# One 128-partition load of the Toeplitz operand in place of two 64-partition loads

## The chip, the cores and the metric

The kernel runs on one core of a Trainium2 chip. The metric is the device time of one execution in microseconds (us). A profile of one execution was taken by the hardware profiler; "the span" is the time from its first to its last instruction. Engines: PE is TensorE, DVE is VectorE, ACT is ScalarE, POOL is GpSimd, SP is SyncE, whose queue issues every transfer of this kernel. Sixteen DMA engines move the data.

## The reference

Two branches read the same x (2048 positions, 448 channels, bfloat16) and are mixed by a gate per position:

```python
g = _sigmoid((x * gate_w).sum(-1, keepdims=True))
a = _A_ref(x, A_wq, A_wk, A_wv, A_wo)      # attention, 16 heads of 28, one shared key and value head
b = _B_ref(x, B_A_re, ..., B_Dskip)        # per channel d: y = causal convolution of x[:, d] with K[d, :], plus x * Dskip
return g * a + (1 - g) * b

# in _B_ref: the convolution's kernel K, 448 channels x 2048 lags, and the convolution itself by FFT
P = jnp.exp(logdA[:, :, None] * l[None, None, :])
K = jnp.einsum("dn,dnl,dn->dl", Cc, P, dB).real
y = irfft2(rfft2(x padded) * rfft2(K padded))[..., :L]
```

## The kernel before, in words

**The scheduler.** All work is given to `Prog` as operations with an engine, an estimated duration, what they read and write, and a priority. `Prog.schedule` simulates the engines with these estimates and writes down a fixed order for each engine; `Prog.emit` adds semaphore waits. At run time every engine works through its own list strictly in order, SP's list of transfers too. In the simulation a transfer takes 60 ns of SP for each of its parts, and then a time that follows from the pair `(rows, bytes per row)`; for a load of T that pair is (128, 8192) before and after the change.

**Attention.** `main` runs over 4 x 4 x 16 x 4 tiles (query chunk, group, key tile, head in the group) in 410 groups of three or two tiles. For each group PE computes scores (L905), ACT takes the exponential (L915) and PE multiplies with the values (L929). After 64 tiles `norm` divides by the sum of the exponentials, which goes through three small transfers (denT, R_scratch, rdenB) on SP's queue and three DVE operations (L874, L879, L883).

**The convolution.** It is done without an FFT, in 28 chunks of 16 channels, spread evenly over the attention's groups by `chunk_step`:

- `tables` (DVE) and `kgen` (PE, L764) compute the chunk's K for all lags; DVE copies it to `kstg` (L774), and four transfers write it to `KP_scratch` in DRAM, one row of 2112 elements for each channel; four channels are interleaved element by element, so that neighbouring lags of one channel are 4 elements apart.
- `tload(gi)` loads for four channels the operand T, a Toeplitz matrix laid out by overlapping reads: partition r of a half holds 4096 elements (8192 bytes) that begin r positions (of 4 elements) later than those of partition 0. There are three buffers for T (`NTR = 3`), and 112 loads in all, 4 per chunk. A load waits for the chunk's transfers to `KP_scratch` and until the buffer's last matmuls are done. It is two transfers of 64 partitions: partitions 64 to 127 begin 4096 elements, or 1024 lags, after partitions 0 to 63.
- `conv(c)` runs two chunks behind `tables(c)`. For each load it issues 64 small matmuls (L820) in 8 operations, of low priority, so that they stand between the attention's matmuls. Their other operand is U, x in blocks of 64 positions; the sum runs over the 128 partitions of U and T. DVE then takes the result out of PSUM (L828), and `ytr` (L797, L804) transposes it and adds it to the output O.

**U** is loaded once (`uload`, 48 transfers of 64 partitions): partitions 0 to 63 hold blocks in one order, partitions 64 to 127 hold the blocks 16 further on, since the second half of T lies 1024 lags away. Where partitions 0 to 63 have no block, U must be zero; a memset in `consts` (L394) sees to that.

**In time.** The first 84 us prepare x, the parameters and the first attention groups. Loads of T run from 84.5 us to 745 us. What remains is attention, the output projection and the stores of O.

Of the kernel before, what the change touches and what calls it, by code (L numbers as in the profile page):

```python
# [11 lines left out]
P = 128  # L12

S = 2048
D = 448
# [8 lines left out]
KPW = 2112  # L24
# [20 lines left out]
def dram(t, off, dims):  # L45
    return bass.AP(tensor=t.tensor, offset=t.offset + off, ap=[list(d) for d in dims])
# [240 lines left out]
class Kernel:  # L287
# [79 lines left out]
    def consts(self):  # L367
        pg = self.pg
        V = lambda b, off, n: b.v(0, P, off, [[1, n]])
        pg.op("pool", lambda e: e.memset(V(self.ident, 0, P), 1.0), 200, wr=["id"])  # L370
        pg.op("pool", lambda e: e.affine_select(
            out=V(self.ident, 0, P), in_=V(self.ident, 0, P), compare_op=ALU.is_equal, fill=0.0,
            base=0, pattern=[[-1, P]], channel_multiplier=1), 300, rd=["id"], wr=["id"])
        sm = self.small
        pg.op("dve", lambda e: e.tensor_reduce(V(sm, 0, 1), self.ident.v(0, P, 28, [[32, 4]]), AX.X, ALU.max),
              100, rd=["id"], wr=["s0"])
        pg.op("dve", lambda e: e.tensor_scalar(V(sm, 1, 1), V(sm, 0, 1), -0.5, 0.5, ALU.mult, ALU.add),
              100, rd=["s0"], wr=["s1"])
        pg.op("dve", lambda e: e.tensor_scalar(V(sm, 2, 1), V(sm, 0, 1), 0.5, 0.5, ALU.mult, ALU.add),
              100, rd=["s0"], wr=["s2"])  # L380
        pg.op("dve", lambda e: e.memset(V(sm, 3, 1), 0.5 * math.pi), 60, wr=["hpi"])
        for c, val in enumerate([-1.0, 1.0, 1.0, -1.0]):
            pg.op("pool", lambda e, c=c, val=val: e.memset(V(self.sgn, c, 1), val), 60, wr=["sgn"])
        ms = lambda buf, n, val, key: pg.op("dve", lambda e: e.memset(V(buf, 0, n), val), 60 + n / 3.8, wr=[key])
        ms(self.Wq, NT * 512, 0.0, "Wq")
        ms(self.Wk, NT * P, 0.0, "Wk")
        pg.op("dve", lambda e: e.memset(self.Wk.v(96, 32, 3 * P + 28, [[32, 4]]), 1.0), 60, wr=["Wk"])
        pg.op("dve", lambda e: e.memset(self.Wk.v(96, 16, 3 * P + 28, [[32, 4]]), 0.0), 60, wr=["Wk"])
        pg.op("dve", lambda e: e.memset(self.xT.v(96, 32, 3 * S, [[1, S]]), 1.0), 600, wr=["xT3a", "xT3b"])
        ms(self.Wo, NT * D, 0.0, "Wo")  # L390
        ms(self.Wb, P, 0.0, "Wb")
        pg.op("dve", lambda e: e.memset(self.vaug.v(0, P, 28, [[32, 16]]), 1.0), 80, wr=["va"])
        pg.op("dve", lambda e: e.memset(self.vaug.v(0, P, 29, [[32, 16], [1, 3]]), 0.0), 80, wr=["va"])
        pg.op("dve", lambda e: e.memset(self.U.v(0, 64, 16 * D, [[1, 16 * D]]), 0.0), 2000, wr=["Uz"])  # L394
        an = self.anti.v(0, 32, 0, [[32, 4], [1, 32]])
        pg.op("pool", lambda e: e.memset(an, 1.0), 100, wr=["anti"], pr=4)
        pg.op("pool", lambda e: e.affine_select(out=an, in_=an, compare_op=ALU.is_equal, fill=0.0, base=-31,
                                                pattern=[[0, 4], [1, 32]], channel_multiplier=1), 300,
              rd=["anti"], wr=["anti"], pr=4)
        pg.op("dve", lambda e: e.memset(V(self.kstg, 0, 256), 0.0), 100, wr=[("kst", 0)])  # L400
# [40 lines left out]
    def uload(self):  # L441
        pg, x = self.pg, self.ins["A_x"]
        for k in range(3):
            lst = []
            for p in range(16):
                if k == 0:
                    hb, pos, blk = 0, p, 15 - p
                else:
                    hb, pos, blk = 1, p + 16 * (k - 1), 31 - p - 16 * (k - 1)
                lst.append((self.U.v(64 * hb, 64, pos * D, [[1, D]]), dram(x, 64 * blk * D, [[D, 64], [1, D]])))  # L450
            pg.dma(lst, (1024, 896), f"u{k}", rd=["sw", "Uz"], wr=["U"], pr=2)

    def bank(self, b, bf=False):
# [327 lines left out]
    def tload(self, gi):  # L781
        pg = self.pg
        s = gi % self.NTR
        c = gi // 4
        pg.dma([(self.T.v(64 * h, 64, s * 4096, [[1, 4096]]),
                 dram(self.KP, 4 * gi * KPW + 4096 * h, [[4, 64], [1, 4096]])) for h in range(2)],
               (128, 8192), f"T{s}", rd=[("KP", c), "pad"], wr=[("T", s)], pr=1)

    def ytr(self, c):
# [246 lines left out]
```

## Time and profile before

| | |
|---|---|
| median of 3 runs | 817.01 us (816.29 to 826.21) |
| the profiled execution's own time | 816.14 us |
| its span | 814.4 us |
| mean granted clock of TensorE | 0.747 |
| busy: PE / DVE / ACT | 636.6 / 530.4 / 506.6 us |
| DMA queue of SP (q1) | 132.60 MB, 72.5% of 16 engines |
| issues of T | 224 of 512 KB |

How to read the lines that follow. "L820" is line 820 of the kernel. A wait is written `engine line <- releaser: us in total, times, longest us`. In the groups, `out<-in` names the buffers, then the shapes, the count, and busy time with the mean of one. PEclk is the clock that TensorE was granted, as a share of full speed. The DMA share is the mean busy share of the 16 DMA engines and can go a little over 1 where packets overlap. A releaser called "issue" means that the engine waited for nothing that the profile shows. Durations come from the one profiled execution.

### The profile page before, as it was taken

The page shows a single profiled execution, that of the slowest core. Times are in us where ns is not written, and L with a number is a line of the kernel's source. Part 1 is how long each engine was busy: PE and PEld are TensorE (multiplying, and loading weights), DVE is VectorE, ACT ScalarE, POOL GpSimd, SP SyncE. Part 2 cuts the span into 40 slices and gives each one's busy share as a digit, 9 for nine tenths or more (in the row PEclk, how much of TensorE's full clock was granted, in tenths as well). Part 3 has the DMA queues.
Part 4 walks back from the last instruction along what each step waited for, and adds up shares of the span by engine and source line. Part 5 has one row for each costly group of instructions (what it writes and reads, how often), then busy time and mean ns, then how long its engine had stood idle before and what let it go on. Part 6 is the DMA issues. An engine that isn't in the chain of part 4 may idle for free.

```text
span 814.4 us, 25556 instructions
## 1 busy us (share of the span) xinstructions
PE 636.6 (78%) x11649; PEld 307.7 (38%) x11649; DVE 530.4 (65%) x1156; ACT 506.6 (62%) x430; POOL 1.6 (0%) x12
## 2 busy tenths in 40 slices
PE   6378888797889878878789978778878988866852
PEld 4212243344334443444443543343433544433211
DVE  7999677956678684956769786755759867300101
ACT  3368667675665755756577856555658766654850
POOL 0000000000000000000000000000000000000000
PEclk9655668687677976868887967775868987876656
DMA  8032883899947899599948799796983799999003
GB/s 209 1 78 59 179 189 85 191 203 209 224 97 165 190 221 225 126 222 210 225 110 201 166 218 221 165 215 136 228 195 95 159 205 214 209 210 214 20 2 103
DMA packets 46036, 134.23 MB, mean 165 GB/s; under 512 B 14968, under 2 KB 29544, under 8 KB 31592
## 3 DMA queue, kind: packets, MB, share of 16 engines
q1 hardware_dynamic: 45928, 132.60, 72.5%
q8 instruction: 91, 1.49, 0.9%
q14 instruction: 17, 0.14, 0.1%
HBM read 128.57 MB, written 3.86 MB: 163 GB/s over the span
## 4 chain that ended last, share of the span: by engine, by line
DMA 38%; PE 38%; DVE 9%; SPq 6%; ACT 5%; issue 4%
DMA T<-KP_scratch 30%; PE psS L820 10%; PE psS L905 9%; PE psB L929 9%; SPq L102 6%; PE psX L764 5%; ACT expT L915 5%; DMA denT<-acc 4%; PE psX L640 2%; DMA rdenB<-R_scratch 2%; DMA R_scratch<-denT 1%; DMA KP_scratch<-kstg 1%; PE psX L851 1%; DVE tab L725 1%; DVE acc L874 1%
## 5 line engine op out<-in xcount | busy, mean ns | idle before, releaser
L915 ACT ACTIVATE expT<-psS 128x1536 bf16<-128x1536 f32 (+1 forms) x410 | 490.7, 1237 | 254.2 <-PE psS L905 247.9
L820 PE MATMUL psS<-T,U 128*32 128x64 bf16 (+15 forms) x7168 | 191.1, 257 | 95.3 <-DMA T<-KP_scratch 70.5
L929 PE MATMUL psB<-expT,vaug 128*32 128x512 bf16 x1024 | 207.4, 494 | 23.4 <-ACT expT L915 18.5
L820 PEld LDWEIGHTS psS<-T,U 128*32 128x32 bf16 (+15 forms) x7168 | 155.5, 182 | 174.3 <-issue 76.6
L905 PE MATMUL psS<-qT,kT 29*128 29x512 bf16 x1024 | 198.1, 484 | 4.2 <-issue 3.8
L905 PEld LDWEIGHTS psS<-qT,kT 29*128 29x128 bf16 x1024 | 39.8, 94 | 147.4 <-issue 146.6
L929 PEld LDWEIGHTS psB<-expT,vaug 128*32 128x32 bf16 x1024 | 53.0, 116 | 71.3 <-ACT expT L915 53.9
L725 DVE TENSOR_TENSOR tab<-tab,mbf 128x2048 bf16<-128x2048 bf16 (+4 forms) x140 | 78.2, 564 | 0.5
L733 DVE TENSOR_TENSOR tab<-tab,tmp 128x128 bf16<-128x128 bf16 (+4 forms) x140 | 77.9, 564 | 0.5
L728 DVE TENSOR_TENSOR tmp<-tab,mbf 128x128 bf16<-128x128 bf16 (+4 forms) x140 | 78.0, 563 | 0.0
L764 PE MATMUL psX<-tab 128*32 128x64 bf16 x1792 | 65.5, 293 | 8.3 <-issue 6.0
L764 PEld LDWEIGHTS psX<-tab 128*32 128x32 bf16 x1792 | 47.8, 140 | 26.6 <-issue 20.3
L828 DVE TENSOR_TENSOR cst<-psS,omq 128x256 bf16<-128x256 f32 x28 | 11.7, 420 | 63.7 <-PE psS L820 63.7
L879 DVE RECIPROCAL denT<-denT 128x16 f32<-128x16 f32 x16 | 4.0, 253 | 54.8 <-DMA denT<-acc 54.6
L883 DVE TENSOR_TENSOR onT<-acc,rdenB 128x512 bf16<-128x512 f32 x16 | 11.0, 690 | 38.9 <-DMA rdenB<-R_scratch 38.9
L874 DVE TENSOR_TENSOR acc<-psB,grow 128x512 f32<-128x512 f32 x16 | 11.0, 689 | 36.4 <-PE psB L929 36.2
L743 DVE TENSOR_TENSOR tmp<-tab,mbf 128x2048 bf16<-128x2048 bf16 x28 | 34.1, 1217 | 0.0
L748 DVE TENSOR_TENSOR tab<-tab,tmp 128x2048 bf16<-128x2048 bf16 x28 | 34.1, 1217 | 0.0
L741 DVE TENSOR_TENSOR tab<-tab,mbf 128x2048 bf16<-128x2048 bf16 x28 | 34.0, 1216 | 0.0
L697 DVE TENSOR_TENSOR mbf<-mst,sgn 128x256 bf16<-128x256 f32 x70 | 29.2, 417 | 0.0
L774 DVE CAST kstg<-psX 128x256 bf16<-128x256 f32 x28 | 11.7, 419 | 22.7 <-PE psX L764 22.5
L646 DVE TENSOR_REDUCE absq<-psX 128x512 bf16<-128x512 f32 x16 | 11.0, 688 | 23.5 <-PE psX L640 23.3
(106 smaller groups left out, 328.7 us busy)
## 6 DMA issues: line engine op xcount, KB each, us to landing
T<-KP_scratch SPq DMA_DIRECT2D x224, 512.0 KB, 9.0
rdenB<-R_scratch SPq DMA_DIRECT2D x64, 64.0 KB, 3.6
U<-in_A_x_dram SPq DMA_DIRECT2D x48, 56.0 KB, 2.2
tab<-in_A_x_dram SPq DMA_DIRECT2D x4, 448.0 KB, 5.0
KP_scratch<-kstg SPq DMA_DIRECT2D x112, 16.0 KB, 4.7
out_dram<-O SPq DMA_DIRECT2D x16, 112.0 KB, 1.8
denT<-acc SPq DMA_DIRECT2D x64, 2.0 KB, 3.7
acc<-in_A_wq_dram SPq DMA_DIRECT2D x1, 392.0 KB, 5.2
```

Of the source, the lines that this page charges most:

```text
L102: return [e.dma_start(o, i, **kw) for o, i in pairs]
L725: pg.op("dve", lambda e, d=dst3, a=src, m=m, w=w: e.tensor_tensor(d, a, mbf.v(0, P, m, [[HC, 4], [0, w], [1, HC]]), ALU.mult), el(n, 1.92) ...
L728: pg.op("dve", lambda e, a=src, m=m, w=w: e.tensor_tensor(tmp.v(0, P, so, [[w * HC, 4], [HC, w], [1, HC]]), a, mbf.v(0, P, m + 128, [[HC, ...
L733: pg.op("dve", lambda e, d=d2, t=t2: e.tensor_tensor(d, d, t, ALU.add), el(n, 1.92), rd=[("tmp", s), ("tab", s, lv + 1)], wr=[("tab", s, l ...
L741: pg.op("dve", lambda e: e.tensor_tensor(dst, src, mbf.v(0, P, m, [[HC, 2], [0, 32], [1, HC]]), ALU.mult), el(n, 1.92), rd=rk + mk, wr=[(" ...
L743: pg.op("dve", lambda e: e.tensor_tensor(tmp.v(0, P, so, [[BLK, 2], [HC, 32], [1, HC]]), src, mbf.v(0, P, m + 64, [[HC, 2], [0, 32], [1, H ...
L748: pg.op("dve", lambda e: e.tensor_tensor(d2, d2, t2, ALU.add), el(n, 1.92), rd=[("tmp", s), ("tab", s, 6)], wr=[("tab", s, 6)], pr=pr)
L764: r = e.matmul(self.psX.v(32 * g, 32, 64 * jj, [[1, 64]]), tab.v(0, P, to + (4 + comp) * BLK + o, [[HC, 32]]), tab.v(0, P, to + comp * BLK ...
L820: r = e.matmul(ps.v(32 * j, 32 - m_, po + 64 * k, [[1, 64]]), self.U.v(0, P, m_ * D + 4 * gi + j, [[D, 32 - m_]]), self.T.v(0, P, s * 4096 ...
L905: r = e.matmul(self.psS.v(0, P, 1536 * s + 512 * k, [[1, 512]]), kT.v(32 * h, DH + 1, 128 * kt, [[1, 128]]), qT.v(32 * h, DH + 1, 512 * qs ...
L915: pg.op("act", lambda e: e.activation(expT.v(0, P, 1536 * es, [[1, n]]), self.psS.v(0, P, 1536 * s, [[1, n]]), AF.Exp, scale=SQ), 172 + n ...
L929: r = e.matmul(self.psB.v(32 * h, 32, 0, [[1, 512]]), vaug.v(0, P, 32 * kt, [[1, 32]]), expT.v(0, P, 1536 * es + 512 * k, [[1, 512]]), sta ...
```

## The change

T's two halves are no longer stacked on partitions 0 to 63 and 64 to 127 but interleaved: partition 2r + h holds row r of half h. One transfer then fills all 128 partitions; its source runs over 64 rows (4 elements apart), 2 halves (4096 elements, that is 1024 lags, apart) and 4096 elements. U is interleaved in the same way, by a partition step of 2 in its loads, so that each matmul sums over the same 128 pairs in another order. The memset of U's second block of columns now covers all 128 partitions, since the partitions that need the zero are no longer contiguous. In the scheduler's simulation a load takes 60 ns of SP where it took 120.

```diff
-        pg.op("dve", lambda e: e.memset(self.U.v(0, 64, 16 * D, [[1, 16 * D]]), 0.0), 2000, wr=["Uz"])
+        pg.op("dve", lambda e: e.memset(self.U.v(0, P, 16 * D, [[1, 16 * D]]), 0.0), 2000, wr=["Uz"])
...
-                lst.append((self.U.v(64 * hb, 64, pos * D, [[1, D]]), dram(x, 64 * blk * D, [[D, 64], [1, D]])))
+                lst.append((bass.AP(tensor=self.U.h, offset=hb * self.U.rs + pos * D, ap=[[2 * self.U.rs, 64], [1, D]]), dram(x, 64 * blk * D, [[D, 64], [1, D]])))
...
-        pg.dma([(self.T.v(64 * h, 64, s * 4096, [[1, 4096]]),
-                 dram(self.KP, 4 * gi * KPW + 4096 * h, [[4, 64], [1, 4096]])) for h in range(2)],
+        pg.dma([(self.T.v(0, P, s * 4096, [[1, 4096]]),
+                 dram(self.KP, 4 * gi * KPW, [[4, 64], [4096, 2], [1, 4096]]))],
                (128, 8192), f"T{s}", rd=[("KP", c), "pad"], wr=[("T", s)], pr=1)
```

## The prediction

> **What bounds the kernel now.** I read the page first, then the PE's list of waits, then stretches of 20 us, then the DMA view of one full stretch.
>
> ```profile
> span 814.4 us, 25556 instructions
> DMA  8032883899947899599948799796983799999003
> q1 hardware_dynamic: 45928, 132.60, 72.5%
> DMA 38%; PE 38%; DVE 9%; SPq 6%; ACT 5%; issue 4%
> ```
>
> The 40 digits are slices of 20.36 us. Seventeen of them show a 9 under DMA: some 346 us in which the 16 DMA engines are full, while the average over the span is only 72.5%. In the chain that ended last, DMA holds as much as TensorE (PE). The next view is the PE's list of waits (what waited, for whom: us in total, times, longest).
>
> ```profile
> engine line waited for: us in total, times, longest us
> PE psS L820 <- DMA T<-KP_scratch: 70.5, 52, 3.3
> PE psB L929 <- ACT expT L915: 18.5, 42, 0.8
> PE psS L820 <- issue: 16.4, 13, 3.2
> ...
> ```
>
> The largest wait of the PE is the convolution (L820) waiting for its Toeplitz operand T. ScalarE (ACT) makes it wait a quarter as long. Now stretches of the span (columns: length, busy us of PE, weight load, DVE, ACT, POOL; then granted clock, DMA share, GB/s):
>
> ```profile
> 0.00:84.00 84.00, 55.94 (x416) 22.92 (x417) 74.27 (x164) 46.26 (x46) 1.59 (x12) 0.66 0.33 85
> 60.00:80.00 20.00, 17.18 (x122) 4.23 (x120) 19.39 (x42) 17.23 (x15) 0.00 (x0) 0.50 0.24 64
> 340.00:360.00 20.00, 14.35 (x299) 6.82 (x290) 12.62 (x27) 9.49 (x8) 0.00 (x0) 0.57 1.01 222
> 420.00:460.00 40.00, 38.12 (x629) 18.71 (x632) 37.68 (x80) 30.68 (x27) 0.00 (x0) 0.87 0.63 143
> 160.00:700.00 540.00, 446.54 (x9093) 228.48 (x9094) 386.65 (x833) 350.10 (x292) 0.00 (x0) 0.78 0.84 187
> 84.00:760.00 676.00, 552.49 (x11092) 277.04 (x11090) 450.64 (x984) 435.62 (x364) 0.00 (x0) 0.77 0.83 184
> ```
>
> From 340 to 360 us the DMA is full at 222 GB/s and every compute engine has room: PE 72%, DVE 63%, ACT 47%. From 420 to 460 us, where the DMA has slack, PE is 95% busy and DVE 94%. So the kernel alternates between being bound by the loads of T and by PE. All 112 loads lie between 84 and 760 us; the first 84 us and the last 54 us are out of the change's reach.
>
> **What a load costs now, and what it may cost.** One load is 128 rows of 8192 bytes, 1.049 MB. The same stretch in the DMA view (share of 16 engines; issues with KB and us to landing), and then 2.7 us near the start, when x is loaded into all 128 partitions:
>
> ```profile
> DMA packets 857, 4.43 MB, mean 222 GB/s; under 512 B 198, under 2 KB 326, under 8 KB 326
> q1 hardware_dynamic: 855, 4.40, 100.3%
> T<-KP_scratch SPq DMA_DIRECT2D x7, 512.0 KB, 8.8
> ```
>
> ```profile
> GB/s 332 345 358 319 385 358 411 385 345 398 358 412 359 372 372 398 385 345 398 372 398 372 372 385 385 372 372 372 319 358 319 332 319 345 332 332 345 319 345 358
> DMA packets 1121, 0.98 MB, mean 361 GB/s; under 512 B 32, under 2 KB 1121, under 8 KB 1121
> q1 hardware_dynamic: 1121, 0.98, 106.8%
> ```
>
> With all engines busy in both, the 64-partition halves of T move 222 GB/s and the 128-partition loads of x 361, though x comes in rows of only 896 bytes. At 222 GB/s a load takes 4.72 us, at 361 it would take 2.90 us. That shape and not row size is the cause is an inference; a second row helps. The 48 loads of U have x's row length but 64 partitions:
>
> ```profile
> DMA packets 3841, 2.77 MB, mean 77 GB/s; under 512 B 768, under 2 KB 3840, under 8 KB 3840
> q1 hardware_dynamic: 3840, 2.76, 29.2%
> U<-in_A_x_dram SPq DMA_DIRECT2D x48, 56.0 KB, 2.2
> ```
>
> Per unit of share U moves 77/0.292 = 264 GB/s and x 361/1.068 = 338: with the same rows, 64 partitions are 1.28 times slower. So the bounds of the new load are 2.90 us (as x) and 4.72/1.28 = 3.69 us. I take 2.90, since x is the only load here that spans 128 partitions.
>
> PE needs 14.35 us per 20 us in the full stretch, that is 14.35/20 x 4.72 = 3.39 us per load. That is more than 2.90, so **PE takes over the pace**. First estimate of the gain: 346 us x (1 - 3.39/4.72) = 97 us, if nothing else ever stands in the way; by the bound 3.69 it is 75 us.
>
> **The change part by part, against the profiled execution (816.14 us, of which 814.4 are the span; the median of the runs is 817.01).**
>
> Waits for T: 70.5 us of PE. I let a tenth stay, for loads that could not be issued early since their buffer came free late: -63. With 3.69 us per load, (4.72 - 3.69)/(4.72 - 3.39) = 77% of the wait goes: -54. Bounds -54 to -70.5.
>
> The 16.4 us of "issue" in front of L820 name no releaser. Some of it may be the landing of the second half. I take half: -8, bounds 0 and -16.4.
>
> Issues on SyncE's queue (SP):
>
> ```profile
> L102 SPq DMA_DIRECT2D T<-KP_scratch x224: 444/596/1540, 84.5 to 744.9; - x112
> L394 DVE MEMSET U<- x1: 3045/3045/3045, 6.8 to 6.8; 64x3584 uint32 x1
> ```
>
> There are 112 issues fewer at a median of 0.596 us, 67 us of SP's time. They are hidden today: the second half is issued while the first half's 512 KB move (2.36 us). Where SP has stood waiting for a free buffer the cover is gone and the last row lands up to 0.6 us sooner, at most 52 x 0.596 = 31 us; that shortens the same waits and is not counted twice. Nothing is moved past another entry of the queue: the issues of KP, denT and rdenB behind a load only come 0.6 us earlier. I don't know the issue time of the three-dimensional source; between 0.6 and twice that, it replaces two such issues and costs nothing more.
>
> The memset of U over 128 instead of 64 partitions takes as many elements per partition, 3.05 us as before, at 6.8 us in the span and long before U's first use. The 48 loads of U keep rows, bytes and count and are paced by SP's issues between 40 and 74 us, while T's first load starts at 84.5: 0. The matmuls sum over the same 128 pairs of rows in another order: 0. No wait is added.
>
> The clock. Two groups of the same three matmuls (start and length in us), in stretches with clocks 1.00 and 0.52:
>
> ```profile
> 400.00:404.00 4.00, 2.61 (x74) 1.55 (x74) 1.63 (x3) 2.86 (x4) 0.00 (x0) 1.00 1.02 229
> 406.00:412.00 6.00, 5.06 (x119) 2.41 (x114) 5.86 (x10) 2.62 (x3) 0.00 (x0) 0.52 1.02 228
> ```
>
> ```profile
> 401.68 0.39 PE L905 MATMUL psS<-qT,kT 29*128 29x512 bf16 x3
> ...
> ```
>
> ```profile
> 406.38 0.61 PE L905 MATMUL psS<-qT,kT 29*128 29x512 bf16 x3
> ...
> ```
>
> So a group costs about 0.39 + 0.22 x (1/clock - 1) us, and the loop over key tiles makes 410 such groups (of three or two) for L905 and 410 for L929. At the mean clock of 0.77 (84 to 760 us) 820 groups hold 54 us of slowness. The full-DMA stretch had 0.57, the free one 0.87. If the mean rises to 0.82, 820 x 0.22 x (1.30 - 1.22) = 14 us go: I take -15. Bounds: -54 if all runs at 1.00, +39 if it falls to 0.66 as before 84 us (820 x 0.22 x (1.515 - 1.299)).
>
> [...]
>
> New waits: PE's order is fixed and its next partner is ACT, for which it waits 18.5 us now; denser, it may wait up to twice as long. I add +12, bounds 0 and +18.5. DVE has 386.65 of 540 us between 160 and 700; 75 us less makes it 83%, and from 420 to 460 us it ran at 94%, so it does not bind yet.
>
> Sum: 816.1 - 63 - 8 - 15 + 12 = 742, and 743 beside the median. It stays below both first estimates (97 and 75 us gained). Its own range, with the clock between +15 and -40 and the other terms at their bounds, is 700 to 785.
>
> **The rivals.**
>
> *The load gets no faster (0.20).* The limit would be something that both shapes share: the source, 64 starts 8 bytes apart in the same 16 KB, or pairs of DMA engines that stay in each other's way. For it: T's source overlaps row by row, x's does not. Against it: U and x, 264 against 338. Only the second issue is gained; a third of its 31 us gives 816.1 - 10 = 806, with the median 807, between 800 and 818. [...]
>
> *The clock falls (0.10).* The DMA is faster, but a denser PE is granted less: 816.1 - 63 - 8 + 39 + 12 = 796. For it: clock 0.50 at 86% busy from 60 to 80 us. Against it: 0.87 at 95% from 420 to 460 us.
>
> *Slower: the load is spread over fewer engines (0.10).* The source's outer dimension has 64 entries, the destination's 128. An engine carries 361/16 = 22.6 GB/s in x's loads. On 8 engines a load takes 1.049/0.181 = 5.8 us, and the 346 full us stretch by 5.8/4.72, +80 us at most: 897, or 857 if half is absorbed elsewhere; I say 880. It decides below 222/22.6 = 9.8 engines. Against it: today's halves, with 64 entries on both sides, keep all 16 full (100.3%).
>
> **How the numbers follow.** The forecast has 0.60. A measurement of this kernel tells about 2% from no change, so faster is below 801 and slower above 833. Faster: all but little of the forecast (0.58), over half of the falling clock (0.06) and a little of the unchanged load (0.03): 0.67. Slower: the fewer engines, 0.10. The same: 0.23. The range 705 to 820 leaves out the slower rival and the forecast's lower edge, some 0.18.
>
> **What would show it.** Right: 112 issues of T of 1024 KB, landing in under 6 us; over 330 GB/s where the share is full; queue q1 near 50% instead of 72.5; the PE's wait for T under 15 us; clock about 0.8. If full stretches still show about 222 GB/s, the load step is wrong. If they show 360 but PE's busy time per load grows past 4 us, the clock step is. If T lands later than 9 us with a share near 0.5, the load runs on half of the engines.

## The result and the profile after

The changed kernel takes 703.0 us (median of 4 runs), the kernel before 819.6 beside it: a ratio of 0.853, 95% interval 0.842 to 0.864. The ratio compares means and leaves out the slowest run of the changed kernel, 706.45 us. The forecast was 743, with a range from 705 to 820. The direction and the place were right, the size was too small: 74 us were forecast, and the medians are 117 us apart. The profiled execution took 703.07 us, of which 701.3 are the span.

The page of the changed kernel, with the lines that answer to those shown of before (span; DMA in 40 slices; the queue; the chain):

```profile
span 701.3 us, 25444 instructions
PE 583.5 (83%) x11649; PEld 304.8 (43%) x11649; DVE 529.3 (75%) x1156; ACT 502.9 (72%) x430; POOL 1.6 (0%) x12
...
DMA  9013167296736588485916587774935377694003
...
q1 hardware_dynamic: 44136, 132.59, 55.8%
...
PE 46%; DMA 22%; DVE 17%; ACT 6%; SPq 4%; issue 3%
...
T<-KP_scratch SPq DMA_DIRECT2D x112, 1024.0 KB, 6.9
```

The same 132.6 MB now fill the DMA engines for 55.8% of a shorter span, and of seventeen slices with a 9 five are left. DMA's part of the chain has gone from 38% to 22%. PE's busy time has fallen from 636.6 to 583.5 us although it executes the same 11649 matmuls. Two stretches in which T keeps the queue nearly full (length, busy us of the engines, granted clock, DMA share, GB/s), and between them the whole time in which loads of T run:

```profile
141.00:159.00 18.00, 16.89 (x442) 10.13 (x430) 15.88 (x34) 14.56 (x13) 0.00 (x0) 0.94 0.93 344
84.00:650.00 566.00, 500.28 (x11113) 274.03 (x11111) 451.41 (x986) 435.93 (x368) 0.00 (x0) 0.92 0.64 221
620.00:636.00 16.00, 14.61 (x374) 8.13 (x370) 1.87 (x4) 13.10 (x11) 0.00 (x0) 0.89 0.97 356
```

With all 16 engines busy T moves 344 to 356 GB/s where it moved 222. A load of 1.049 MB takes about 3.0 us (1.049/0.350). And the clock: in the time of the loads the mean is 0.92, where it was 0.77. The PE's waits of the changed kernel:

```profile
PE psS L820 <- DMA T<-KP_scratch: 25.4, 23, 3.0
PE psB L929 <- ACT expT L915: 20.1, 47, 0.8
PE psS L820 <- issue: 10.4, 11, 1.9
```

The wait for T has shrunk from 70.5 to 25.4 us, the unnamed one before L820 from 16.4 to 10.4. The wait for ACT is 20.1, where it was 18.5. Of the signs that the prediction named, the 112 issues of 1024 KB and the rate over 330 GB/s are there; a load lands after 6.9 us, not under 6, and the wait for T is not under 15.

The scheduler's order is the same for PE, DVE, ACT and POOL; on SP's queue a pair of issues has become one. So nothing in the 113 us between the two profiled spans comes from another order of these engines.

### The profile page after: what moved, and what is told of

It is laid out like the page before. It is cut to its first block, busy times and chain, and to the rows that moved or that the text cites. A ratio compares the mean times of both kernels' runs of the same rounds, so it can differ in the third digit from the quotient of the medians.

```text
span 701.3 us, 25444 instructions
## 1 busy us (share of the span) xinstructions
PE 583.5 (83%) x11649; PEld 304.8 (43%) x11649; DVE 529.3 (75%) x1156; ACT 502.9 (72%) x430; POOL 1.6 (0%) x12
## 3 DMA queue, kind: packets, MB, share of 16 engines
q1 hardware_dynamic: 44136, 132.59, 55.8%
## 4 chain that ended last, share of the span: by engine, by line
PE 46%; DMA 22%; DVE 17%; ACT 6%; SPq 4%; issue 3%
PE psS L820 15%; DMA T<-KP_scratch 14%; PE psS L905 11%; PE psB L929 10%; PE psX L764 5%; ACT expT L915 5%; SPq L102 4%; DMA denT<-acc 4%; DMA rdenB<-R_scratch 3%; PE psX L640 2%; DMA R_scratch<-denT 2%; DVE tab L733 2%; DVE tab L725 2%; DVE tmp L728 1%; PE psX L851 1%
## 5 line engine op out<-in xcount | busy, mean ns | idle before, releaser
L820 PE MATMUL psS<-T,U 128*20 128x64 bf16 (+15 forms) x7168 | 187.0, 254 | 42.4 <-DMA T<-KP_scratch 25.4
L929 PE MATMUL psB<-expT,vaug 128*32 128x512 bf16 x1024 | 183.7, 439 | 25.0 <-ACT expT L915 20.1
L820 PEld LDWEIGHTS psS<-T,U 128*20 128x20 bf16 (+15 forms) x7168 | 154.4, 182 | 102.8 <-issue 60.9
L905 PE MATMUL psS<-qT,kT 29*128 29x512 bf16 x1024 | 176.0, 430 | 0.5 <-ACT expT L915 0.5
L905 PEld LDWEIGHTS psS<-qT,kT 29*128 29x128 bf16 x1024 | 39.1, 93 | 120.2 <-issue 119.1
L764 PE MATMUL psX<-tab 128*32 128x64 bf16 x1792 | 64.7, 293 | 5.5 <-DVE tab L748 3.6
L764 PEld LDWEIGHTS psX<-tab 128*32 128x32 bf16 x1792 | 47.5, 140 | 21.3 <-issue 11.4
L828 DVE TENSOR_TENSOR cst<-psS,omq 128x256 bf16<-128x256 f32 x28 | 11.8, 420 | 28.8 <-PE psS L820 28.7
L883 DVE TENSOR_TENSOR onT<-acc,rdenB 128x512 bf16<-128x512 f32 x16 | 11.1, 692 | 25.1 <-DMA rdenB<-R_scratch 25.0
L685 DVE TENSOR_TENSOR msq<-mst 128x256 f32<-128x256 f32 x63 | 26.6, 422 | 0.0
L879 DVE RECIPROCAL denT<-denT 128x16 f32<-128x16 f32 x16 | 4.0, 253 | 27.4 <-DMA denT<-acc 27.4
```

The lines of the kernel that those rows point to most:

```text
L764: r = e.matmul(self.psX.v(32 * g, 32, 64 * jj, [[1, 64]]), tab.v(0, P, to + (4 + comp) * BLK + o, [[HC, 32]]), tab.v(0, P, to + comp * BLK ...
L820: r = e.matmul(ps.v(32 * j, 32 - m_, po + 64 * k, [[1, 64]]), self.U.v(0, P, m_ * D + 4 * gi + j, [[D, 32 - m_]]), self.T.v(0, P, s * 4096 ...
L905: r = e.matmul(self.psS.v(0, P, 1536 * s + 512 * k, [[1, 512]]), kT.v(32 * h, DH + 1, 128 * kt, [[1, 128]]), qT.v(32 * h, DH + 1, 512 * qs ...
L929: r = e.matmul(self.psB.v(32 * h, 32, 0, [[1, 512]]), vaug.v(0, P, 32 * kt, [[1, 32]]), expT.v(0, P, 1536 * es + 512 * k, [[1, 512]]), sta ...
```

## The experiments

Two theories stood at the start. **Supply**: the change makes T's loads faster, and everything else (waits, clock, DVE) follows from T being in time. **Layout**: the interleaving or the single issue does something of its own. Where an experiment's order on PE, DVE and ACT is not that of the changed kernel, it is said.

### What makes a load fast

**Two transfers again, but interleaved.**

```diff
-        pg.dma([(self.T.v(0, P, s * 4096, [[1, 4096]]),
-                 dram(self.KP, 4 * gi * KPW, [[4, 64], [4096, 2], [1, 4096]]))],
+        pg.dma([(bass.AP(tensor=self.T.h, offset=h * self.T.rs + s * 4096, ap=[[2 * self.T.rs, 64], [1, 4096]]),
+                 dram(self.KP, 4 * gi * KPW + 4096 * h, [[4, 64], [1, 4096]])) for h in range(2)],
```

> The interleaved layout, but each load is again two transfers: half 0 to the even partitions, half 1 to the odd ones (64 rows each, partition step 2). If it is enough that a transfer reaches across all 128 partitions, T moves at 340 to 360 GB/s as after the change and the time is 700 to 715 us. If the rate belongs to one transfer of 128 rows, T moves at about 222 GB/s as before and the time is 805 to 825 us. The loads of U after the change, which have this same step and count, moved 74/0.299 = 247 GB/s per unit of share, no more than the 264 of before, so the second is the likelier.

Measured: 703.4 us, ratio to before 0.862 (0.856 to 0.867), clock 0.861. The expectation that was called the likelier is refuted. Its DMA view from 140 to 160 us:

```profile
GB/s 344 459 426 393 442 410 410 459 328 162 94 203 246 393 279 82 279 377 131 147 328 311 377 344 279 393 410 426 426 426 459 279 344 361 459 365 219 146 66 8
q1 hardware_dynamic: 1313, 6.17, 81.7%
T<-KP_scratch SPq DMA_DIRECT2D x8, 512.0 KB, 6.0
```

There are two issues of 512 KB for each load, as before the change, reading the same bytes in the same order as before the change. Only the partitions differ that each of them writes. The slices of 0.5 us reach 459 GB/s; the mean is 312/0.831 = 375 per unit of share (6.24 MB in 20 us, 81.7% for SP's queue and 1.4% for the others). So a load of T was fast here when each transfer reached across the 128 partitions, be it in every second one (375 GB/s per unit of share, where stacked halves had 222/1.01 = 220); the number of transfers does not matter here, and the 67 us of SP's issue time that the change saves are worth nothing that can be measured (703.0 and 703.4).

The records of single packets say the same. Of the 8192-byte packets of T the median takes

```text
before 609 ns    after 309 ns
```

that is, twice as long before as after. The run further down that leaves out the second half of T still moves 126 GB/s at a share of 0.55, which is 229 per unit of share, so it does not take both halves: here a transfer to 64 neighbouring partitions was slow by itself. Why it was slow, no run here shows.

**One transfer without interleaving.**

```diff
-        pg.dma([(self.T.v(64 * h, 64, s * 4096, [[1, 4096]]),
-                 dram(self.KP, 4 * gi * KPW + 4096 * h, [[4, 64], [1, 4096]])) for h in range(2)],
+        pg.dma([(self.T.v(0, P, s * 4096, [[1, 4096]]),
+                 dram(self.KP, 4 * gi * KPW, [[4096, 2], [4, 64], [1, 4096]]))],
```

> The stacked layout of before, in one transfer of 128 partitions whose source runs over 2 halves, 64 rows and 4096 elements. If the number of DMA engines follows from the outermost dimension of both sides, it is 2 here; with 22.6 GB/s for each engine (x's loads, 361/16) a load takes 23 us, 112 loads 2600 us, and the time is 2500 to 2900 us. If the split follows the 128 partitions alone, the interleaving was not needed and the time is that of the changed kernel, 700 to 715 us.

Measured: 2446 us, in one run. From 400 to 1400 us:

```profile
DMA packets 12199, 54.38 MB, mean 54 GB/s; under 512 B 3498, under 2 KB 5050, under 8 KB 5930
q1 hardware_dynamic: 12155, 53.71, 13.2%
T<-KP_scratch SPq DMA_DIRECT2D x50, 1024.0 KB
```

54 GB/s at 13.2% of 16 engines, which is 2.1 engines: by this estimate two are at work, each at 27 GB/s (the estimate of 22.6 was low, which is why the time is just under the expected 2500). So the interleaving is not decoration. The outermost dimension of the source has two entries, and the load kept two engines busy at a time. With 64 rows outermost and 2 halves inside, as after the change, SP's queue fills 92.0 and 96.6% of the 16 engines in the two full stretches.

### What lateness of T costs

**Half of T's rows, stacked as before.** The edit: `for h in range(2)` became `for h in range(2 if gi < self.NTR else 1)`.

> The kernel before, but from the fourth load on only the first half of T (partitions 0 to 63) is loaded; lags of the second half are left out of the result in effect, the matmuls are all there. A load then moves half of the bytes, still at the slow rate: 2.36 us. If the whole gain of the change comes from T being in time, this kernel gains the same: PE waits for T under 25 us, clock 0.86 or more, time 690 to 705 us. If the interleaved layout or the wide transfer does anything else for the time, it stays above 730 us.

Measured: 674.3 us, ratio 0.826 (0.823 to 0.829), clock 0.864, the PE's wait for T 7.4 us. That is faster than the 690 to 705 expected: a load of half the bytes takes 2.36 us by the rate of before, where the changed kernel's takes 3.0. The old layout with half the bytes is faster than the new one with all of them. The gain is one of supply, and it doesn't end at 703.

**The changed kernel with ballast on the DMA queue.**

```diff
...
-        pg.dma([(self.T.v(0, P, s * 4096, [[1, 4096]]),
-                 dram(self.KP, 4 * gi * KPW, [[4, 64], [4096, 2], [1, 4096]]))],
+        src = lambda w: dram(self.KP, 4 * gi * KPW, [[4, 64], [4096, 2], [1, w]])
+        pg.dma([(self.T.v(0, P, s * 4096, [[1, 4096]]), src(4096)), (dram(self.BAL, gi * 128 * 2048, [[2048, 128], [1, 2048]]), src(2048))],
```

> The changed kernel, with a second transfer behind every load that copies 0.52 MB from DRAM to DRAM, so that 1.57 MB go with every load and T comes about as late as before (4.4 to 5 us per load at 320 to 360 GB/s). If late T makes both the waits and the low clock, the waits for T return to 55 to 90 us, the clock falls to 0.74 to 0.79 and the time is 790 to 830 us. If the clock has another cause, the waits return but the clock stays at 0.85 and the time stays below 770 us.

Measured: 794.1 us, ratio 0.972 (0.967 to 0.977), clock 0.774. T and its ballast share a semaphore, so the wait bears the ballast's name:

```profile
PE psS L820 <- DMA BAL_scratch<-KP_scratch: 77.3, 49, 4.2
PE psB L929 <- ACT expT L915: 19.0, 46, 0.8
...
```

With the new layout and a late T both come back, the waits (77.3 us) and the low clock, as the supply theory expected. Some 23 us to the kernel before remain (794.1 against 816.8 beside it); a load with its ballast is still a little faster, 4.5 us by the estimate in the table below against 4.7. Layout as the theory for the main part of the gain is out; a small effect of its own is not.

**An eighth of T's columns.** The edit: `[1, 4096]` on both sides became `[1, w]`, with `w = 4096 if gi < self.NTR else 512`.

> The changed kernel, but from the fourth load on only 512 of 4096 columns of T are loaded (one eighth of the bytes; the result is computed with stale columns). Order of every engine as in the changed kernel. It shows what T's lateness still costs after the change. If the 25.4 us of waits and the clock that goes with them are all that is left, the PE's wait for T is under 8 us, the clock 0.86 to 0.89 and the time 668 to 680 us, as with half of the rows (674). If a load's 2 us or so of latency, not its bytes, keeps the waits, the time stays at 695 to 705.

Measured: 648.1 us, ratio 0.789 (0.784 to 0.794), clock 0.878; the PE's wait for T is 0.4 us. The expectation of 668 to 680 was too slow, and by the same mistake as the forecast: it counted the 25.4 us of waits and little else. DVE's waits for the small transfers of the normalisation fall with it, for denT from 27.4 us after the change to 22.3, for rdenB from 25.0 to 12.2.

### What sets the granted clock

**Half of the convolution's matmuls.** The edit, on top of the eighth of T: `for m_ in (m, m + 1)` became `for m_ in (m,)`, with the group's end at 14.

> As the run with an eighth of the columns, and half of the convolution's matmuls left out (32 in place of 64 for each load). T is in time, so no wait lowers the clock. If the granted clock follows only from the waits of the PE for T, it stays at 0.86 or above, PE's busy time falls by some 90 us and the time is 590 to 625 us. If it follows from how densely the array is used, with the convolution's 128-row matmuls keeping it up (attention alone had 0.50 at 86% busy between 60 and 80 us), the clock falls to 0.60 to 0.75, and with it the matmuls of attention take longer: 620 to 660 us.

Measured: 640.4 us, ratio 0.778 (0.773 to 0.784), clock 0.814. The stretch from 84 to 600 us, with an eighth of T, and then with half of the matmuls as well:

```profile
84.00:600.00 516.00, 489.05 (x11117) 272.12 (x11114) 449.30 (x986) 435.46 (x368) 0.00 (x0) 0.95 0.21 48
```

```profile
84.00:600.00 516.00, 468.52 (x7570) 214.66 (x7567) 447.39 (x986) 439.95 (x376) 0.00 (x0) 0.85 0.21 47
```

T is in time in both (PE waits 0.4 and 3.7 us for it), yet the clock falls from 0.95 to 0.85 when a third of the matmuls goes, and attention's matmuls get longer (L905 from 422 to 448 ns). Leaving out 3584 matmuls is worth 8 us. PE also idles more, which could be the cause instead. The run with half of T's rows speaks against that: between 84 and 620 us its PE is busy just as much, 91% of the time, at a clock of 0.92:

```profile
84.00:620.00 536.00, 487.99 (x11052) 271.16 (x11065) 446.55 (x979) 427.97 (x361) 0.00 (x0) 0.92 0.55 126
```

So the clock went here with what PE is given to do (0.95 with all of the convolution's matmuls, 0.85 with half of them) as well as with its waits for T (a mean of 0.862 after the change, 0.774 with the ballast). The fall to 0.60 to 0.75 that this theory expected was too deep; the first theory's 0.86 and more doesn't hold either.

### Where the rest of the lateness comes from

Two kernels moved transfers to GpSimd's queue, by `eng="pool"` in the calls of `norm` or of `tload`.

> The changed kernel, with the normalisation's three small transfers (denT, R_scratch, rdenB) issued from GpSimd's queue. On SyncE's queue the loads of T then no longer stand behind transfers that wait for DVE (after the change SP waits 50.5 us for DVE's acc and 24.2 for denT). If part of the remaining 25.4 us of waits for T comes from loads that were issued late, 8 to 15 us go and the time is 685 to 697 us. If the loads are held up by their own buffers and by KP_scratch alone, nothing moves (700 to 706), and if the transfers from GpSimd take longer, DVE waits for denT and rdenB more than the 52.4 us of now and the time is 705 to 720.

> The changed kernel, with the loads of T issued from GpSimd's queue, all other transfers from SyncE's. Neither stands behind the other any more: a load is issued as soon as its buffer is free and its rows of KP_scratch are written, and denT, R_scratch and rdenB never stand behind a load's wait. If late issue is what is left of the waits, the time is 675 to 695 us, with PE's wait for T under 15 us. If issuing from GpSimd is slow, T lands later than 6.9 us after its issue and the time is 705 or more.

Measured: 722.3 us (ratio 0.878, 0.872 to 0.885) and 722.0 us (0.871, 0.862 to 0.880). The first is slower than the change, and than all that was expected of it. The second is not faster, and whether it is slower is open: its four runs lie between 710 and 730 us, and its interval overlaps that of the change. The PE's wait for T does fall, to 15.9 and 20.8 us, but another takes its place. The first of the two:

```profile
PE psS L820 <- DVE cst L828: 17.3, 5, 5.5
PE psS L820 <- DMA T<-KP_scratch: 15.9, 17, 2.5
...
```

```profile
DVE onT L883 <- DMA rdenB<-R_scratch: 38.6, 10, 6.5
DVE cst L828 <- PE psS L820: 34.4, 13, 8.1
DVE denT L879 <- DMA denT<-acc: 34.1, 14, 5.9
...
```

DVE's order is fixed, and it waits 72.7 us for denT and rdenB (52.4 after the change); L828, which frees the convolution's bank of PSUM, stands behind. The second kernel's profile, of a run of 725 us, has 38.3 and 35.6 us, although there no load of T stands on SP's queue. Slow landing is not the reason as far as the medians go: denT and rdenB land 1.9 and 2.4 us after their issue in the first kernel (2.2 and 2.2 after the change), and T lands after 6.7 us in the second (6.9). Whether the issue from GpSimd or the earlier loads of T delay them, these runs don't tell apart.

Then four buffers for T, with a control for the smaller tmp and absq that make room (orders on PE and DVE differ from the changed kernel's):

```diff
-        self.absq = sb("absq", 2 * 512, BF)
+        self.absq = sb("absq", 512, BF)
...
-        self.tmp = sb("tmp", 2 * 2048, BF)
-        self.NTR = 3
+        self.tmp = sb("tmp", 2048, BF)
+        self.NTR = 4
...
```

> The changed kernel with four buffers for T in place of three; the room comes from one buffer in place of two for tmp (DVE) and for absq. The scheduler's order on PE and DVE differs from the changed kernel's, so a control with the same smaller buffers and three for T runs beside it. If T is still late because a load cannot start until a buffer is free, the PE's wait for T falls from 25.4 us to under 12, and the time is 10 to 35 us below the control's (the run with an eighth of T's bytes had 648 us). If the loads wait for KP_scratch and for their turn on SyncE's queue, both kernels have the same time within 8 us.

> The control: the changed kernel with one buffer for tmp and one for absq, T with three buffers as it is. DVE works in order and needs one tmp at a time, so what is expected is the changed kernel's time, 695 to 710 us. A difference beyond that is the price of another order, and has to be taken off whatever four buffers bring.

Measured: 704.7 us against the control's 716.6, with waits for T of 22.7 and 37.2 us. The fourth buffer is worth 12 us, at the edge of what was expected, though the wait stays well above the 12 us expected. But the control is 13.6 us slower than the changed kernel, also more than expected: all in all nothing is gained.

Last, the order. The scheduler simulates a load as 2.5 us of transfer and 2.2 us of latency; the trace has a median of 6.9 us from issue to landing.

```diff
-    DMA_NS = 2200
+    DMA_NS = 4400
```

> The changed kernel, with the scheduler's latency of a transfer set to 4400 ns in place of 2200 (nothing but the fixed order changes). The profile has a median of 6.9 us from issue to landing, the scheduler counts 2.5 + 2.2 us. If the remaining waits for T come from an order that expects T too early, PE's waits for T fall under 15 us and the time is 680 to 698 us. If they come from the buffers, the time stays at 697 to 710 us.

Measured: **648.4 us**, ratio to before 0.792 (0.787 to 0.796), clock 0.901, far under the 680 to 698 expected. It is the fastest kernel here with the whole of the work. Its waits:

```profile
PE psB L929 <- ACT expT L915: 21.7, 49, 1.6
...
PE psS L820 <- issue: 4.9, 9, 1.3
...
PE psS L820 <- DMA T<-KP_scratch: 4.3, 5, 1.3
```

The loads land as they did (6.8 us after their issue); PE comes to L820 when T is there. The two waits before L820 are 26.6 us shorter than after the change, PE's idle time in all is 31 us and its busy time 22.5 us shorter. The latency counts for every transfer in the simulation, so the order around denT and rdenB moved too (DVE's waits for them fall from 52.4 to 25.1 us); what this adds is not separated. The kernel reaches the time of the kernel that loads an eighth of T. Is it then the order alone? The same edit on the kernel before, with the same order on PE, DVE and ACT:

> The kernel before (stacked halves, two transfers) with the scheduler's latency at 4400 ns: PE, DVE and ACT have the same order as in the changed kernel with 4400 ns, only the layout of T and U differs. The DMA alone needs 112 x 4.72 = 529 us for T at 222 GB/s; with 84 us ahead of the loads and 54 us behind them that is a floor of 667 us. If the order was what held the kernel up and not the rate of the loads, the time comes close to that floor, 670 to 700 us. If the rate is what counts, waits for T of 40 us and more stay, the clock stays under 0.82 and the time is 730 to 790 us.

Measured: 767.4 us, ratio 0.937 (0.931 to 0.944), clock 0.807. Its waits before L820:

```profile
PE psS L820 <- DMA T<-KP_scratch: 42.7, 33, 3.1
PE psS L820 <- issue: 36.3, 19, 3.5
```

At 222 GB/s this order does not hide the loads: the time is 100 us above its floor of 667, as expected for the case that the rate counts. With that order the layout is worth 767.4 - 648.4 = 119 us, with the old one 117 (819.6 - 703.0). The two edits hardly depend on each other.

All kernels but the one of 2446 us that have the whole convolution and leave every transfer on its queue, by the time that the DMA needs per load (bytes per load over 222, or over 350 GB/s; waits are PE's before L820, DMA + issue):

| kernel | us per load | waits, us | mean clock | time, us |
|---|---|---|---|---|
| before | 4.7 | 70.5 + 16.4 | 0.747 | 819.6 |
| ballast | 4.5 | 77.3 + 2.8 | 0.774 | 794.1 |
| before, latency 4400 | 4.7 | 42.7 + 36.3 | 0.807 | 767.4 |
| after | 3.0 | 25.4 + 10.4 | 0.862 | 703.0 |
| three buffers, smaller tmp and absq | 3.0 | 37.2 + 5.9 | 0.850 | 716.6 |
| four buffers, smaller tmp and absq | 3.0 | 22.7 + 12.8 | 0.846 | 704.7 |
| two interleaved | 3.0 | 31.2 + 4.1 | 0.861 | 703.4 |
| half of the rows | 2.4 | 7.4 + 6.4 | 0.864 | 674.3 |
| after, latency 4400 | 3.0 | 4.3 + 4.9 | 0.901 | 648.4 |
| an eighth of the columns | 0.4 | 0.4 + 0 | 0.878 | 648.1 |

Between the first and the last row the waits before L820 fall by 86 us and the time by 171. The clock's order isn't strictly that of the time, and it is not the only other thing that moves: PE's total idle time (span less busy) is 178 us before, 118 after and 80 with an eighth of T.

## Why the prediction was right or wrong

**The load (right).** 2.90 us were forecast from x's loads; T moves 344 to 356 GB/s in full stretches, 3.0 us. That the destination's partitions are the cause is now shown by the two interleaved transfers, where it had been an inference.

**The evidence from U (wrong, without effect).** U's lower rate, 264 GB/s per unit of share, was read as a sign of its 64 partitions. After the change U's loads reach across all partitions and still move 74/0.299 = 247:

```profile
DMA packets 3703, 2.68 MB, mean 74 GB/s; under 512 B 736, under 2 KB 3702, under 8 KB 3702
q1 hardware_dynamic: 3702, 2.66, 29.9%
```

So their pace does not come from the partitions, and the upper bound of 3.69 us had no ground. U had also been the evidence against the rival that the load gets no faster; as far as U goes, it was luck that this rival did not come true.

**Waits for T (place right, too large).** Forecast -63, measured 25.4 - 70.5 = -45. The tenth that was to stay is over a third. The step behind it was that "PE needs 14.35 us per 20 us in the full stretch, that is 14.35/20 x 4.72 = 3.39 us per load", for which a load of 2.90 us comes in time. But 3.39 us is what PE did per load while T held it up. Over the whole time of the loads PE was busy 552.49/112 = 4.93 us per load before and 500.28/112 = 4.47 us after, so on average even the old load of 4.72 us was not slower than PE, and the estimate of 97 us was no ceiling. What waits stay hangs on when the fixed order asks for each load: with another order the wait is 4.3 us.

**"Issue"**: forecast -8, measured -6.0. **SP's issues, memset, U**: forecast nothing; two interleaved transfers give the same time with the 112 issues back.

**The clock (this term failed).** The step was: "If the mean rises to 0.82 [...] 14 us go: I take -15". The mean between 84 us and the end of the loads rose from 0.77 to 0.92. By the formula of the prediction 820 x 0.22 x (1/0.77 - 1/0.92) = 38 us; PE's busy time in all fell by 636.6 - 583.5 = 53 us, of which attention's two groups of matmuls have 46. So the rise of the clock was set too low, and the formula gives too little for the rise as well: -53 is almost the -54 that it had for a clock of 1.00 throughout. That the clock rose because T is in time is shown by the ballast, which takes most of the rise back with the new layout in place (means over the span: 0.747 before, 0.862 after, 0.774 with the ballast). The groups show it (columns after the bar: busy us, mean ns of one):

```profile
L929 PE MATMUL psB<-expT,vaug 128*32 128x512 bf16 x1024 | 207.4, 494 | 23.4 <-ACT expT L915 18.5 <-DVE omq L627 4.0 <-issue 0.4
L905 PE MATMUL psS<-qT,kT 29*128 29x512 bf16 x1024 | 198.1, 484 | 4.2 <-issue 3.8 <-ACT expT L915 0.5
L820 PE MATMUL psS<-T,U 128*32 128x64 bf16 (+15 forms) x7168 | 191.1, 257 | 95.3 <-DMA T<-KP_scratch 70.5 <-issue 16.4 <-DVE cst L828 5.9
```

```profile
L820 PE MATMUL psS<-T,U 128*20 128x64 bf16 (+15 forms) x7168 | 187.0, 254 | 42.4 <-DMA T<-KP_scratch 25.4 <-issue 10.4 <-DVE cst L828 4.6
L929 PE MATMUL psB<-expT,vaug 128*32 128x512 bf16 x1024 | 183.7, 439 | 25.0 <-ACT expT L915 20.1 <-DVE omq L627 4.0 <-DVE acc L874 0.2
L905 PE MATMUL psS<-qT,kT 29*128 29x512 bf16 x1024 | 176.0, 430 | 0.5 <-ACT expT L915 0.5
```

The first three rows are before, the last three after: the matmuls of attention, which the change doesn't touch, are 11% shorter. The prediction had this at hand. It had a free stretch at 0.87 beside the full one at 0.57; by its formula 0.87 gives -27 and a sum of 730. For a falling clock it had one row, 60 to 80 us, where PE was 86% busy at clock 0.50. That row was of another mix, attention and some matmuls of L764 without any of L820, and after the change the same stretch still has 0.50:

```profile
60.00:80.00 20.00, 17.19 (x108) 3.89 (x105) 20.00 (x48) 17.18 (x15) 0.00 (x0) 0.50 0.29 70
```

The run with half of the convolution shows why it could not speak for the rest. With T in time the clock was 0.95 with all of the convolution's matmuls and 0.85 with half. What keeps the stretch from 60 to 80 us at 0.50, no run here shows.

**New waits (too large).** Forecast +12 for ACT, measured 20.1 - 18.5 = +1.6. A denser PE did not wait for ACT, since ACT too had been idle 248 us for PE's scores and still is for 135. Other waits shrank instead, DVE's own above all (for denT from 54.6 to 27.4 us): PE's idle time fell by 60 us, of which the two waits before L820 are 51.

The sum by terms: -45 - 6 - 53 + 1.6 and about -10 of other idle time give the -113 of the profiled executions; forecast had been -63 - 8 - 15 + 12. The prediction gave its own range as 700 to 785; its terms at the bounds that it names add up to 689 (816.1 - 70.5 - 16.4 - 40) and 796 (816.1 - 54 + 15 + 18.5), so that range was too narrow.

**The rivals.** "The load gets no faster" did not happen: the split of 64 x 2 rows against 128 does no harm (344 to 356 GB/s), and even 64 rows two partitions apart run at that rate (375 GB/s per unit of share). "The clock falls" is refuted, it rose. "Fewer engines" did not happen here, but it did in the run with one transfer and no interleaving: with the 2 outermost about two engines were at work (54 GB/s at 13.2% of 16) and it took 2446 us.

## What to carry to other kernels

Where a load fills part of the partitions, look at which ones: 64 rows in every second partition moved 1.7 times as fast here as 64 neighbouring ones (375 against 220 GB/s per unit of share), for no more than an operand permuted on both sides of the sum. Keep a large dimension outermost in the source of a transfer (64 entries kept 92.0 and 96.6% of the 16 engines busy here, 2 entries 13.2%, which is two of them). And when a wait of PE goes, count the matmuls that the clock makes shorter as a term of its own, with a clock read from a stretch of the same mix of matmuls that is free of that wait; then look whether the fixed order still expects the transfer earlier than it lands.

## What the runs showed of the hardware beyond that

- Transfers whose source has 2 entries outermost moved 54 GB/s at 13.2% of 16 engines, by estimate two engines at 27 GB/s each.
- In the clock records of the two profiled executions, before and after, the granted clock has only two values, 0.5 and 1 (74 and 40 stretches). A mean of 0.77 is full clock for 54% of the time, 0.92 for 84%.
- At an unchanged order, 3584 matmuls of the convolution less shortened the time by 8 us only: the clock fell from 0.95 to 0.85 between 84 and 600 us, and PE idled 97 us in all instead of 80.
- Moving the small transfers of the normalisation to GpSimd's queue cost about 19 us (722 against 703), and DVE's waits for denT and rdenB grew from 52.4 us to 72.7. Moving the loads of T there gained nothing (710 to 730 us).
